# A row of maxima in another PSUM ring and one step earlier, the first weight loads three steps later, and a split of weights without its shift

## The chip, the cores and the metric

The kernel runs on one core of one Trainium2 chip. The time is device microseconds (us) of one launch. A profiled execution gives the trace, in which PE is TensorE's matmuls, PEld its weight loads, DVE is VectorE, ACT is ScalarE, POOL is GpSimd and SP is the engine that issues the DMAs.

## The reference

Attention with rotary positions, then two feed-forward layers, on float32 data (the weights of the layers come as float64 and are read as pairs of 32-bit words):

```
B, H, S, D = 4, 8, 576, 64                      # 32 heads
q, k = rotate(q), rotate(k)
scores = q @ k.T / sqrt(D)
attn = exp(scores - max(scores)) / (sum + 1e-9)
x = attn @ v                                    # to 2304 tokens x 512
x = (sigmoid(x @ w_gate) * (x @ w_val)) @ w_out      # 512 -> 1536 -> 512
x = elu(x @ w_in) @ w_out2                           # 512 -> 2048 -> 512
```

## The kernel before, in words

Products that need more than the fast matmul's precision are made of three: high by high, high by low part, low by high. So each operand is split into a high part (a cast on ACT) and a low part (a difference on DVE or POOL).

**Attention.** The order of the work is written out by hand as an agenda. A slot is one head (32 of them), and a slot has ten steps. In each step PE makes one tile of scores for head i (`scores`, L448: two matmuls into one bank of the ring `ps_qk`, of three banks), one tile of raw scores for head i+2 whose row maxima DVE takes (`maxima`, L400, ring `ps_mt` of two banks), and one step of the product with v for the scores of five steps ago (`values`, L475). ACT turns each tile of scores into its exponential (L468), which frees the bank. In steps 4 and 9 the tile is a tail of 64 rows; ACT writes its exponential twice (L465 and, in place, L468) and DVE takes a difference (`low_part`, L471, a step and a half later), which frees that bank. `at(slot, step, f)` puts f behind the work of a step; a step of ".5" puts it ahead of the next step's scores. What is put at one step goes out in the order in which the `at` calls stand.

**The maxima's row.** `join` (L416, at step 0 of the slot before) brings the maxima of a head together in MJ, `max_row` (L428) turns them into a row by a matmul with the identity (L434), DVE casts the row to SBUF (L436), and SP sends it by DMA into the operand W that the scores of the next head read (L441, or L443 and L444). For heads from 4 on this stands at step 2.5. Its bank is the one bank of `ps_t`, which for pairs of heads from 4 on also takes the transposes of rotated q and k (`split`, L324; T, L337) at steps 4 and 9, whose casts are L344 (ACT) and L340 (DVE).

**Weights.** A generator (`split_all`, L148) loads the float64 weights by halves (L99, 512 KB each) and splits each word by DVE operations (L121 to L140), a cast on ACT and two operations on POOL. For the first chunk each `pull` issues one DVE operation: 14 pulls a half. The first pull issues two loads, and stands at step 0 of slot 5; two pulls a slot follow, at steps 2 and 5 of slots 6 to 29, and the rest one a step from slot 30 on. Later chunks are split during the feed-forward layers, by 8 pulls a half.

**Feed-forward layers.** PE works through tokens in blocks of 512, with two rings of four banks; DVE adds each product to an accumulator (y L728, z L762), which frees the bank.

Of the kernel before, what the change touches and what calls it, by code (L numbers as in the profile page):

```python
# [9 lines left out]
F32 = mybir.dt.float32  # L10
F32R = mybir.dt.float32r
AF = mybir.ActivationFunctionType
ALU = mybir.AluOpType
AX = mybir.AxisListType
I32 = mybir.dt.int32
I64 = mybir.dt.int64


@with_exitstack
def attention_moe_moe_kernel(  # L20
# [15 lines left out]
    nc = tc.nc  # L36
    B, H, S, D = q.shape
    P = 128
# [55 lines left out]
    def load_w(c, n, half):  # L94
        w, view, parts = chunks[c][n]
        n2 = parts // 2
        place = sum(len(halves(j)) for j in range(1, c)) + 2 * n + half
        t = pools["raw", c > 0 and place % 4 > 1].tile([P, n2, DM if view is by_f else FC], I64, tag="raw", name=f"raw{c}_{n}{half}")
        nc.sync.dma_start(out=t, in_=view(w, c if c < NC1 else c - NC1)[:, half * n2 : (half + 1) * n2])  # L99
        raw_w[c, n, half] = t  # L100

    def split_w(c, n, half):

        t = raw_w.pop((c, n, half))
        shape = [P, 2 * t.shape[1], t.shape[2]]
        if half == 0:
            hi = pools["w", c % 2].tile(shape, F32R, tag="wh", name=f"wh{c}_{n}")
            lo = pools["w", c % 2].tile(shape, F32R, tag="wl", name=f"wl{c}_{n}")
            weights.setdefault(c, []).append((hi, lo))
        flat = lambda a: a.rearrange("p k f -> p (k f)")  # L110
        words = flat(t).bitcast(I32).rearrange("p (f two) -> p f two", two=2)
        size = NK * FC // 2
        for j in range(0, size, WP):
            low, high = words[:, j : j + WP, 0], words[:, j : j + WP, 1]
            h, l = (flat(x)[:, half * size + j : half * size + j + WP] for x in weights[c][n])
            e = pools["cv"].tile([P, WP], I32, tag="e", name=f"ce{c}_{n}{half}_{j}")
            m = pools["cv"].tile([P, WP], I32, tag="m", name=f"cm{c}_{n}{half}_{j}")
            a = pools["cv"].tile([P, WP], F32, tag="a", name=f"ca{c}_{n}{half}_{j}")
            mf = m.bitcast(F32)

            nc.vector.tensor_scalar(e, high, 20, 0x7FF, op0=ALU.logical_shift_right, op1=ALU.bitwise_and)  # L121
            if c == 0:
                yield
            nc.vector.tensor_scalar(m, high, 0x07FFFFFF, 3, op0=ALU.bitwise_and, op1=ALU.logical_shift_left)
            yield
            nc.vector.scalar_tensor_tensor(
                m, in0=high, scalar=-0x40000000, in1=m, op0=ALU.bitwise_and, op1=ALU.bitwise_or
            )
            if c == 0:
                yield  # L130
            nc.vector.scalar_tensor_tensor(a, in0=e, scalar=896.5, in1=mf, op0=ALU.is_gt, op1=ALU.mult)  # L131
            yield

            nc.vector.tensor_single_scalar(e, low, 8, op=ALU.logical_shift_right)
            if c == 0:
                yield
            nc.vector.tensor_single_scalar(m, a.bitcast(I32), -0x00800000, op=ALU.bitwise_and)  # L137
            nc.scalar.copy(h, a)  # L138
            yield
            nc.vector.scalar_tensor_tensor(mf, in0=e, scalar=2.0**-44, in1=mf, op0=ALU.mult, op1=ALU.mult)  # L140
            nc.gpsimd.tensor_tensor(out=a, in0=a, in1=h.bitcast(F32), op=ALU.subtract)  # L141
            yield
            nc.gpsimd.tensor_tensor(out=l, in0=a, in1=mf, op=ALU.add)  # L143

    def halves(c):
        return [(c, n, half) for n in range(len(chunks[c])) for half in range(2)] if c < NCH else []

    def split_all(which, ring):  # L148

        for one in which[:ring]:  # L150
            load_w(*one)
        yield
        for n, one in enumerate(which):
            yield from split_w(*one)
            if n + ring < len(which):
                load_w(*which[n + ring])
        yield
# [28 lines left out]
    with ExitStack() as att:  # L186
# [11 lines left out]
        ps_qk = banks.enter_context(tc.tile_pool(name="ps_qk", bufs=3, space=bass.MemoryType.PSUM))  # L198
        ps_t = banks.enter_context(tc.tile_pool(name="ps_t", bufs=1, space=bass.MemoryType.PSUM))
# [88 lines left out]
        def at(slot, step, fn, *args):  # L288
            agenda.setdefault(slot * NSTEP + step, []).append((fn, args))
# [3 lines left out]
        def rope_ops(pr, which, eng):  # L293


            if which == "t":
                x = raw(pr, "kq")
                r = rope_p.tile([P, 2, D], F32, tag="rt", name=f"rt{pr}")
                s = rope_p.tile([P, 2, D], F32, tag="st", name=f"st{pr}")
                rv, sv = r, s  # L300
                cos, sin = (tabt[:, j].unsqueeze(1).to_broadcast([P, 2, D]) for j in range(2))
            else:
                x = raw(pr, which)
                r = rope_p.tile([P, ST, 2, D], F32, tag="r" + which, name=f"r{which}{pr}", bufs=2)
                s = rope_p.tile([P, ST, 2, D], F32, tag="s", name=f"s{which}{pr}")
                rv, sv = (y.rearrange("p t h d -> p h t d") for y in (r, s))
                cos, sin = (tab[:, c].unsqueeze(1).to_broadcast([P, 2, ST, D]) for c in range(2))
            rot[pr, which] = r
            tt = eng.tensor_tensor

            axes = "p n" if which == "t" else "p h t"
            two = lambda y: y.rearrange(f"{axes} (two d) -> {axes} two d", two=2)
            tt(out=two(sv), in0=two(x)[..., ::-1, :], in1=two(sin), op=ALU.mult)
            yield
            tt(out=rv, in0=x, in1=cos, op=ALU.mult)
            yield
            tt(out=r, in0=r, in1=s, op=ALU.add)
            yield
# [97 lines left out]
        def join(i):  # L416
            pr, ab = divmod(i, 2)
            c = slice(ST + 1, 2 * ST + 1) if ab else slice(0, ST + 1)
            nc.vector.tensor_reduce(
                out=MJ[pr % 2][:, c], in_=MX[pr % 2][:, :, c].rearrange("p a t -> p t a"), axis=AX.X, op=ALU.min  # L420
            )
# [6 lines left out]
        def max_row(i):  # L428
            pr, ab = divmod(i, 2)
            mj = MJ[pr % 2]  # L430
            if i == 0:
                join(i)
            m = ps_t.tile([P, 512], F32, tag="t", name=f"mr{i}")[:, 0:P]
            nc.tensor.matmul(m, lhsT=mj[:, ST * ab : ST * ab + P], rhs=ident_r, start=True, stop=True)  # L434
            row = s_p.tile([ST + 1, P], F32R, tag="row", name=f"row{i}")
            nc.vector.tensor_copy(row, m[0 : ST + 1])  # L436
            z = D * (1 - ab)
            w, src = W[pr % NPAR][ab][z : z + 1, 3 * S :].bitcast(F32), row.bitcast(F32)
            by_p = lambda x: x.rearrange("o (t p) -> o t p", p=P)
            if ab == 0:  # L440
                nc.sync.dma_start(out=by_p(w), in_=src)  # L441
            else:
                nc.sync.dma_start(out=by_p(w[:, 0:SM]), in_=src[1 : ST + 1])  # L443
                nc.sync.dma_start(out=w[:, SM:S], in_=src[0:1, TL:P])  # L444
# [103 lines left out]
        for i in range(1, NHEAD):  # L548
            at(i - 1, 0, join, i)
        for i in range(NHEAD):  # L550
            at(*((i - 2, 9) if i == 0 else (i - 1, 1.5 if i < 4 else 2.5)), max_row, i)

        for qt in QT + MJ:
            at(-6, 0, nc.vector.memset, qt.bitcast(F32), 0.0)
# [4 lines left out]
        for pr, which, eng in ((0, "k", nc.vector), (0, "t", nc.gpsimd), (0, "q", nc.vector), (1, "k", nc.gpsimd), (1, "t", nc.gpsimd), (1, "q", nc.gpsimd)):  # L559
            gen = rope_ops(pr, which, eng)  # L560
# [18 lines left out]
        for pr in range(NPAIR):  # L579
            s0 = 2 * pr  # L580
            if pr > 1:
                for j, (which, slot, steps) in enumerate(
# [6 lines left out]
                    gen = rope_ops(pr, which, nc.gpsimd)  # L589
# [33 lines left out]
            at(NHEAD - 2, 1 + 2 * kk, lambda: pull(split_x[0]))  # L623

        gen = split_all(halves(0), 2)
        at(5, 0, pull, gen)
        pulls = 14 * len(halves(0)) + 1
        early = [(slot, step) for slot in range(6, NHEAD - 2) for step in (2, 5)]
        for slot, step in early:
            at(slot, step, pull, gen)  # L630
# [4 lines left out]
        for n in range(-6 * NSTEP, NHEAD * NSTEP + half_slot):  # L635
            i, h = divmod(n, NSTEP)
# [132 lines left out]
    for c in range(NCH):  # L769

        hooks = (4 + 4) * NB if c < NC1 else 2 * NB + NT // P
        pulls = 8 * len(halves(c + 1)) + 1
# [65 lines left out]
```

## Time and profile before

| | |
|---|---|
| median of 3 runs | 1174.69 us (1174.68 to 1175.4) |
| profiled execution, own time | 1177.32 us |
| its span, first to last instruction | 1175.5 us |
| busy: PE, DVE, ACT, POOL | 1141.1, 933.1, 448.9, 605.3 us |
| granted TensorE clock, mean | 0.999 of full speed (2.4 GHz) |

The attention takes the first 328 us or so, the two layers the rest. Busy time of PE is near the whole span; what counts is where PE waits and for whom.

### The profile page before, as it was taken

The page shows a single profiled execution, that of the slowest core. Times are in us where ns is not written, and L with a number is a line of the kernel's source. Part 1 is how long each engine was busy: PE and PEld are TensorE (multiplying, and loading weights), DVE is VectorE, ACT ScalarE, POOL GpSimd, SP SyncE. Part 2 cuts the span into 40 slices and gives each one's busy share as a digit, 9 for nine tenths or more (in the row PEclk, how much of TensorE's full clock was granted, in tenths as well). Part 3 has the DMA queues.
Part 4 walks back from the last instruction along what each step waited for, and adds up shares of the span by engine and source line. Part 5 has one row for each costly group of instructions (what it writes and reads, how often), then busy time and mean ns, then how long its engine had stood idle before and what let it go on. Part 6 is the DMA issues. An engine that isn't in the chain of part 4 may idle for free.

```text
span 1175.5 us, 16864 instructions
## 1 busy us (share of the span) xinstructions
PE 1141.1 (97%) x5728; PEld 962.9 (82%) x5728; DVE 933.1 (79%) x1994; ACT 448.9 (38%) x1037; POOL 605.3 (51%) x695
## 2 busy tenths in 40 slices
PE   5999999999999999999999999999999999999998
PEld 4887887788888888888888888888888888888887
DVE  6768778878776897767777677688999999999844
ACT  4666666666754332212222122344322222222221
POOL 8665758564243554434444445675545544544521
PEclk9999999999999999999999999999999999999999
DMA  6567676765312111111111111011111101110004
GB/s 168 145 157 179 151 181 140 186 153 133 80 48 94 54 54 55 37 54 37 54 37 47 44 37 36 18 37 54 38 52 37 54 36 55 36 47 9 1 36 126
DMA packets 58758, 88.03 MB, mean 75 GB/s; under 512 B 18176, under 2 KB 30736, under 8 KB 58672
## 3 DMA queue, kind: packets, MB, share of 16 engines
q1 hardware_dynamic: 58672, 86.96, 27.5%
q8 instruction: 45, 0.74, 0.3%
q14 instruction: 41, 0.34, 0.1%
HBM read 55.45 MB, written 4.87 MB: 51 GB/s over the span
## 4 chain that ended last, share of the span: by engine, by line
PE 76%; DVE 17%; ACT 3%; POOL 2%; issue 1%; DMA 1%; SPq 1%; POOLq 0%; ACTq 0%
PE h L680 12%; PE h L679 12%; PE h L681 12%; PE o L679 8%; PE o L680 8%; PE o L681 8%; PE pv L491 6%; PE s L461 5%; DVE z L762 3%; DVE MX L414 2%; PE mt L412 2%; DVE g L705 1%; DVE g L704 1%; DVE ca L131 1%; DVE hl L340 1%
## 5 line engine op out<-in xcount | busy, mean ns | idle before, releaser
L711 POOL TENSOR_TENSOR gl<-g,gh 128x512 fp32r<-128x512 f32 (+1 forms) x140 | 168.6, 1204 | 330.1 <-ACT gh L710 263.8
L710 ACT CAST gh<-g 128x512 fp32r<-128x512 f32 (+1 forms) x140 | 81.0, 579 | 307.6 <-DVE g L705 171.0
L461 PE MATMUL s<-W 128*128 128x288 f32 (+1 forms) x640 | 186.5, 371 | 3.0 <-DMA W<-row 1.7
L680 PE MATMUL h<-xl,wh 128*128 128x512 f32 (+1 forms) x480 | 176.6, 368 | 0.0
L679 PE MATMUL h<-xh,wh 128*128 128x512 f32 (+1 forms) x480 | 176.6, 368 | 0.0
L681 PE MATMUL h<-xh,wl 128*128 128x512 f32 (+1 forms) x480 | 176.5, 368 | 0.0
L414 DVE TENSOR_REDUCE MX<-mt 128x1 f32<-128x288 f32 x288 | 127.0, 449 | 50.5 <-PE mt L412 49.3
L491 PE MATMUL pv<-e,VF 128*128 128x288 f32 x512 | 166.5, 408 | 0.0
L141 POOL TENSOR_TENSOR ca<-ca,wh 128x256 f32<-128x256 f32 x136 | 111.3, 818 | 98.1 <-DVE cm L137 75.6
L461 PEld LDWEIGHTS s<-W 128*128 128x128 f32 (+1 forms) x640 | 109.9, 183 | 28.8 <-ACT e L468 2.6
L138 ACT CAST wh<-ca 128x256 fp32r<-128x256 f32 x136 | 55.1, 405 | 194.9 <-DVE ca L131 194.9
L468 ACT ACTIVATE e<-s 128x288 f32<-128x288 f32 x256 | 104.5, 412 | 43.3 <-PE s L461 40.4
L143 POOL TENSOR_TENSOR wl<-ca,cm 128x256 fp32r<-128x256 f32 x136 | 110.9, 815 | 18.8 <-DVE cm L140 13.0
L680 PE MATMUL h<-yl,wh 128*128 128x512 f32 (+1 forms) x320 | 117.7, 368 | 0.0
L681 PE MATMUL h<-yh,wl 128*128 128x512 f32 (+1 forms) x320 | 117.7, 368 | 0.0
L679 PE MATMUL h<-yh,wh 128*128 128x512 f32 (+1 forms) x320 | 117.7, 368 | 0.0
L679 PE MATMUL o<-wh,gh 128*128 128x512 f32 x288 | 112.7, 391 | 1.4 <-DVE z L762 1.1
L700 DVE TENSOR_TENSOR g<-h,g 128x512 f32<-128x512 f32 (+1 forms) x60 | 38.2, 636 | 94.9 <-PE h L681 92.1
L680 PE MATMUL o<-wl,gh 128*128 128x512 f32 x288 | 112.2, 390 | 0.0
L681 PE MATMUL o<-wh,gl 128*128 128x512 f32 x288 | 112.1, 389 | 0.0
L680 PEld LDWEIGHTS h<-xl,wh 128*128 128x128 f32 x480 | 90.5, 189 | 15.0
L681 PEld LDWEIGHTS h<-xh,wl 128*128 128x128 f32 x480 | 90.5, 189 | 15.0
(110 smaller groups left out, 2521.9 us busy)
## 6 DMA issues: line engine op xcount, KB each, us to landing
W<-hl SPq DMA_DIRECT2D x90, 288.0 KB
raw<-in_moe_w_out_dram SPq DMA_DIRECT2D x28, 512.0 KB
raw<-in_moe_w_in_dram SPq DMA_DIRECT2D x16, 512.0 KB
raw<-in_moe_w_gate_dram SPq DMA_DIRECT2D x12, 512.0 KB
raw<-in_moe_w_val_dram SPq DMA_DIRECT2D x12, 512.0 KB
rb<-d SPq DMA_DIRECT2D x32, 144.0 KB
k<-in_k_dram SPq DMA_DIRECT2D x16, 256.0 KB
q<-in_q_dram SPq DMA_DIRECT2D x16, 256.0 KB
```

Of the source, the lines that this page charges most:

```text
L138: nc.scalar.copy(h, a)
L141: nc.gpsimd.tensor_tensor(out=a, in0=a, in1=h.bitcast(F32), op=ALU.subtract)
L143: nc.gpsimd.tensor_tensor(out=l, in0=a, in1=mf, op=ALU.add)
L414: nc.vector.tensor_reduce(out=MX[pr % 2][:, a, c : c + 1], in_=m, axis=AX.X, op=ALU.max, negate=True)
L461: nc.tensor.matmul(s, lhsT=operand(i, st, t * P, n), rhs=operand(i, mv, a * HS, HS), start=st == "K1", stop=st == "K2")
L468: nc.scalar.activation(e, s, AF.Exp, scale=SCALE)
L491: nc.tensor.matmul(out_ps, lhsT=VF[par][:, ab, t], rhs=e, start=t == 0, stop=False)
L679: nc.tensor.matmul(ps, lhsT=ah, rhs=bh, start=j == 0, stop=False)
L680: nc.tensor.matmul(ps, lhsT=ah, rhs=bl, start=False, stop=False)
L681: nc.tensor.matmul(ps, lhsT=al, rhs=bh, start=False, stop=j == n - 1)
L710: nc.scalar.copy(hi, g)
L711: nc.gpsimd.tensor_tensor(out=lo, in0=g, in1=hi.bitcast(F32), op=ALU.subtract)
```

## The change

Four edits. The row's matmul takes a bank of the scores' ring `ps_qk` in place of `ps_t`. For all heads from 1 on it stands at step 1.5 (it was 2.5 for heads from 4 on). The shift of the low word (L134) goes: the operation behind it reads the low word in place, as an unsigned number, with the scale 2^-52 in place of 2^-44 (the eight low bits were cut off before, and are now kept). So a half takes 12 pulls, and the generator's first pull moves from step 0 to step 3 of slot 5; the later loads of the first chunk then come in slots 12, 18, 24 and 30 (they came in slots 13, 20, 27 and 30).

```
-            nc.vector.tensor_single_scalar(e, low, 8, op=ALU.logical_shift_right)
-            if c == 0:
-                yield
             nc.vector.tensor_single_scalar(m, a.bitcast(I32), -0x00800000, op=ALU.bitwise_and)
             nc.scalar.copy(h, a)
             yield
-            nc.vector.scalar_tensor_tensor(mf, in0=e, scalar=2.0**-44, in1=mf, op0=ALU.mult, op1=ALU.mult)
+            nc.vector.scalar_tensor_tensor(
+                mf, in0=low.bitcast(U32), scalar=2.0**-52, in1=mf, op0=ALU.mult, op1=ALU.mult
+            )
...
-            m = ps_t.tile([P, 512], F32, tag="t", name=f"mr{i}")[:, 0:P]
+            m = ps_qk.tile([P, 512], F32, tag="qk", name=f"mr{i}")[:, 0:P]
...
-            at(*((i - 2, 9) if i == 0 else (i - 1, 1.5 if i < 4 else 2.5)), max_row, i)
+            at(*((i - 2, 9) if i == 0 else (i - 1, 1.5)), max_row, i)
...
-        at(5, 0, pull, gen)
-        pulls = 14 * len(halves(0)) + 1
+        at(5, 3, pull, gen)
+        pulls = 12 * len(halves(0)) + 1
```

PE's order in slot 17 before, from the scores of step 2 to the transpose of step 4 (s_2 is the tile of scores of step 2, mr the row's matmul, Tk the transpose; a name in brackets is whose semaphore the row waits for):

```order
L461 MATMUL s_2_2826<-W_163 128x288 [waits Activation_49]
L461 MATMUL s_2_2826<-W_163 128x288
L412 MATMUL mt_2_2830<-W_165 128x288 [waits DVE_49]
L491 MATMUL pv_1_2800<-e_7_2749,VF_166 128x288
L434 MATMUL mr_2837<-identr,MJ_173 128x128 [waits DVE_49,PE_49]
L461 MATMUL s_3_2843<-W_163 128x288 [waits Activation_49]
L461 MATMUL s_3_2843<-W_163 128x288
L412 MATMUL mt_3_2847<-W_165 128x288 [waits DVE_49]
L491 MATMUL pv_1_2800<-e_8_2761,VF_166 128x288
L337 MATMUL Tk_0_2853<-ident,rk_2664 128x128 [waits DVE_49,Pool_49]
```

The same place in the changed kernel:

```order
L434 MATMUL mr_2825<-identr,MJ_173 128x128 [waits DVE_49,Activation_49]
L461 MATMUL s_2_2831<-W_163 128x288 [waits Activation_49]
L461 MATMUL s_2_2831<-W_163 128x288
L412 MATMUL mt_2_2835<-W_165 128x288
L491 MATMUL pv_1_2800<-e_7_2749,VF_166 128x288
L461 MATMUL s_3_2844<-W_163 128x288 [waits DVE_49]
L461 MATMUL s_3_2844<-W_163 128x288
L412 MATMUL mt_3_2848<-W_165 128x288 [waits DVE_49]
L491 MATMUL pv_1_2800<-e_8_2761,VF_166 128x288
L337 MATMUL Tk_0_2854<-ident,rk_2669 128x128 [waits PE_49,Pool_49]
```

The row's matmul stands ahead of the scores of step 2, and waits for ACT too, since its bank was one of scores; the transpose no longer waits for DVE. In the ring of three banks, one is held by the tail of the step before until DVE's difference, and the row now takes one: by the values that the semaphores wait for, s_2 takes the bank of s_1, and waits for the exponential of step 1 (it waited for that of step 0). In the slots 3, 6, 8, 12, 16, 20, 24 and 28 to 30 it takes the tail's bank, and waits for DVE's difference. From s_3 on the banks are two or more tiles old again, as before.

SP's order in slot 5, before (rk, hl and row are sources in SBUF, raw the weights as they come):

```order
L99 DMA raw_00_1082<-in_moe_w_gate_dram 128x2x256
L99 DMA raw_01_1084<-in_moe_w_gate_dram 128x2x256
L521 DMA r_1032<-d_1_1031 128x9
L441 DMA W_164<-row_1114 1x5x128
L524 DMA d_1_1031<-r_1032 128x9
```

And changed:

```order
L441 DMA W_164<-row_1100 1x5x128
L521 DMA r_1032<-d_1_1031 128x9
L100 DMA raw_00_1123<-in_moe_w_gate_dram 128x2x256
L100 DMA raw_01_1125<-in_moe_w_gate_dram 128x2x256
L524 DMA d_1_1031<-r_1032 128x9
```

The row of head 6 and the sums r go out ahead of the two loads of weights; the reciprocals (d from r) stay behind them.

## Rows read from the trace of the kernel before

**Rows 1.** By stage: length, busy us (x instructions) of PE, PEld, DVE, ACT, POOL, clock, DMA.

```profile
28.00:328.00 300.00, 285.46 (x1685) 244.61 (x1685) 233.23 (x594) 196.52 (x525) 179.51 (x237) 1.00 0.62 149
328.00:850.00 522.00, 522.00 (x2520) 441.38 (x2519) 402.88 (x808) 156.39 (x316) 255.17 (x269) 1.00 0.15 46
850.00:1075.00 225.00, 223.61 (x1038) 186.17 (x1038) 212.98 (x434) 60.50 (x128) 113.56 (x121) 1.00 0.13 43
```

**Rows 2.** Waits, 28 to 330 us: us in total, times, longest.

```profile
PE Tk L337 <- DVE row L436: 5.4, 10, 1.3
PE Tq L337 <- DVE row L436: 4.4, 7, 1.1
...
DVE r L523 <- DMA r<-d: 4.0, 3, 3.5
...
PE s L461 <- DMA W<-row: 1.7, 2, 1.5
...
PE Tq L337 <- POOL st L313: 1.1, 2, 0.7
```

**Rows 3.** Timeline of slot 17: start, duration, engine, line, operation.

```profile
192.71 0.64 PE L461 MATMUL s<-W 128*128 128x288 f32 x2
192.78 0.15 DVE L419 TENSOR_REDUCE MJ<-MX 128x5 fp32r<-128x10 f32 x1
192.81 0.41 ACT L468 ACTIVATE e<-s 128x288 f32<-128x288 f32 x1
...
193.59 0.44 PE L434 MATMUL mr<-identr,MJ 128*128 128x128 f32 x1
...
193.86 0.47 PE L461 MATMUL s<-W 128*128 128x288 f32 x2
...
194.84 0.27 DVE L436 CAST row<-mr 5x128 fp32r<-5x128 f32 x1
...
195.25 0.30 PE L337 MATMUL Tk<-ident,rk 128*128 128x128 f32 x1 [0.30 <-DVE row L436]
...
196.43 0.30 PE L412 MATMUL mt<-W 128*128 128x288 f32 x1
```

**Rows 4.** The same view, slot 22.

```profile
241.97 0.65 PE L461 MATMUL s<-W 128*128 128x288 f32 x2
...
242.29 0.83 ACT L468 ACTIVATE e<-s 128x288 f32<-128x288 f32 x2
```

**Rows 5.** The same view, slot 8.

```profile
104.42 0.45 DVE L471 TENSOR_TENSOR p<-s,p 64x288 fp32r<-64x288 f32 x1
...
104.80 0.65 PE L461 MATMUL s<-W 128*128 128x288 f32 x2
...
107.89 0.43 DVE L414 TENSOR_REDUCE MX<-mt 128x1 f32<-128x288 f32 x1
...
108.11 0.30 PE L337 MATMUL Tq<-ident,rq 128*128 128x128 f32 x1 [1.06 <-DVE row L436]
```

**Rows 6.** The same view, slots 5 and 6.

```profile
76.82 1.37 SPq L99 DMA_DIRECT2D raw<-in_moe_w_gate_dram  x1
...
80.44 0.82 SPq L441 DMA_DIRECT2D W<-row  x1
...
84.45 0.19 PEld L461 LDWEIGHTS s<-W 128*128 128x128 f32 x1 [1.69 <-DMA W<-row]
```

**Rows 7.** One line's instructions (L134, L140, L126): duration ns min/median/max, first and last start.

```profile
L134 DVE TENSOR_SCALAR ce<-raw x136: 275/284/1358, 106.7 to 1104.6; 128x256 int32<-128x256 int32 x136
...
L140 DVE SCALAR_TENSOR_TENSOR cm<-ce,cm x136: 407/426/1543, 116.8 to 1105.6; 128x256 f32<-128x256 int32 x136
...
L126 DVE SCALAR_TENSOR_TENSOR cm<-raw,cm x136: 406/426/1539, 97.2 to 1102.1; 128x256 int32<-128x256 int32 x136
```

**Rows 8.** Waits, 850 to 1160 us.

```profile
PE o L679 <- DVE z L762: 1.1, 2, 0.9
...
PE o L679 <- ACT g L703: 0.3, 1, 0.3
```

More of the change, by code (lines that the diff above doesn't have):

```diff
@@ L16 @@
 I64 = mybir.dt.int64
+U32 = mybir.dt.uint32
 @with_exitstack
```

## The prediction, made before the changed kernel was run

> **What bounds the kernel now.** I read the busy time by stage first. PE is busy without a gap from 328 to 850 us, and waits 1.4 us in all between 850 and 1075; in the attention it waits 14.5 of 300 us, and DVE there is 78% busy [rows 1]. So PE sets the end everywhere, and an edit is worth what it takes from PE's waits or adds to them. The waits by name come next: of the 14.5 us, 9.8 us in 17 waits are transposes T that wait for DVE's cast of the maxima's row, and two more waits of 1.1 us are put down to POOL, but sit at the same instruction; 1.7 us are scores that wait for the DMA of such a row [rows 2]. Last I read the timeline of three slots, to see what stands around that row. In slot 17 the row's matmul starts at 193.59, but DVE casts it at 194.84 only, behind the maxima of step 2 and an operation on weights; the cast ends at 195.11, and T, which needs the same bank, starts at 195.25 [rows 3]. From the end of an operation on another engine to PE's start it is thus 0.14 us; I use that below.
>
> **The change part by part.** The sum is made against the profiled execution (1177.32 us, its span 1175.5 and 1.8 around it). The runs' median, 1174.69, is 2.6 us below; I take the difference over to it.
>
> *The row leaves T's bank.* T then finds its bank free since the last transpose, five steps back. What goes: 5.4 + 4.4 + 1.1 = 10.9 us, 19 waits [rows 2]. What is late next there? T also needs POOL's rotated operand, issued ahead of it by several steps; and PE's next need of DVE is the maximum of step 3, whose bank the raw scores of step 5 take. In slot 8, the longest but one of these waits, T started at 108.11, and that maximum ran from 107.89 to 108.32 [rows 5]; with 0.14 it lets PE go on at 108.46. The raw scores of step 5 come 1.18 us behind T (195.25 to 196.43 [rows 3]), so T may come as early as 107.28 before DVE holds PE there instead. That caps the gain of one slot at 0.83 us. Only two slots reach it: this one (1.06) and the longest (1.3, less the new wait below). Cost of the cap: 0.2 + 0.1 = 0.3 us.
>
> *The row enters the scores' ring, a step earlier.* Now the scores of step 2 follow the row's matmul and take the bank of the scores of step 1, so they wait for ACT's exponential of step 1. In slot 17: they started at 192.71; the row's matmul ahead of them costs 0.27 (193.59 to 193.86), which it cost behind them before, so they want to start at 192.98. The exponential runs from 192.81 to 193.22, and lets them go at 193.36: a wait of 0.38 us [rows 3]. The row's own wait ends up at the same moment: MJ is ready at 192.93, the matmul could go at 193.07 and the scores at 193.34. In slot 22 the first of the two exponentials ends at 242.29 + 0.83/2 = 242.70; they want to go at 242.24 and may at 242.84: 0.60 us [rows 4]. I went through all slots in that way. Twelve odd slots (5, 7, 9 and so on to 27) are like slot 17, 0.33 to 0.39 each; six even ones (4, 10, 14, 18, 22, 26) are like slot 22, 0.57 in the mean; ACT is later there because its cast of the transposed k is larger. In the other slots the bank is that of the tail, and DVE's difference is in time: in slot 8 it ends at 104.87, which gives 105.01, and the scores want 104.80 + 0.27 = 105.07 [rows 5]. So the new wait is 12 x 0.38 + 6 x 0.57 = 8.0 us. Nothing hides it, since all of PE's later work stands behind the scores. No such wait is in the trace. From below it is bounded by nothing, as in the slots of slot 8's kind; from above by two whole exponentials more in each of the 18 slots, 18 x 2 x 0.41 = 14.8, so 22.8 us. I take 8.0, since up to the scores of step 1 both kernels issue the same work, and the exponential's end is read, not guessed. The cast of the row moves ahead of one maximum and the operation on weights on DVE; nothing else there changes place.
>
> *The first loads.* In slot 5 the two loads (1 MB) were issued from 76.82 on, the row of head 6 behind them at 80.44, and the scores that read it were held until 84.45, PE for 1.5 us [rows 6]. Now the row, cast about 76.5, and the sums r go first. That wait goes, and with it DVE's 3.5 us for r [rows 2], during which PE went on. The other 0.2 us of the 1.7 came behind a later load, which now comes after the row too. So 1.7 us go. What is queued behind the loads now: the reciprocals' store and the moves of pair 4, which PE first reads a full slot later, some 9 us, against the 3.6 us that the row took behind the same loads, measured from its issue (80.44 to 84.0). The loads of slots 12, 18 and 24 stand behind that slot's row and ahead of the broadcast of reciprocals, on which POOL alone waits. I cost this at nothing; were the broadcast late, POOL's rotations would be, which are about a slot ahead of T.
>
> *No shift.* 136 operations of DVE go; the middle one takes 284 ns, so at least 38.6 us of DVE. The operation that now reads the low word with a step of two words had a contiguous source; another of its kind that already reads with that step takes the same 426 ns [rows 7]. The unsigned reading is not in the trace: at best it costs nothing, at worst as much as the shift gave, 38.6 us of DVE. I take nothing. On the path that sets the end this counts only where PE waits for DVE in the layers: 1.1 + 0.3 us [rows 8], where DVE is 95% busy [rows 1]; the shifts are spread from 106.7 to 1104.6 us [rows 7], so that far more of their 38.6 us falls into that stage than PE waits there. So 1.4 us go at most, and I take them; otherwise the relief is hidden beside PE. In the attention the number of DVE operations a slot stays at two.
>
> The sum: -10.9 + 0.3 + 8.0 - 1.7 - 1.4 = -5.7 us, so 1171.6 for a profiled execution, and **1169.0 us** beside the median.
>
> The Trainium skill (Perfetto Trace Analysis, Optimization Strategy) says that a gap which repeats on the engine that should be saturated can mean that there are too few buffers for the next tile. It speaks against putting one more tile into a ring of three, and for the second rival below; the trace of before bears it out for a ring of one, by the 17 waits of T.
>
> **The rivals.**
>
> *The new wait doesn't bind.* If the exponential of step 1 is done in time, the 8.0 us stay away: -13.7, 1161.0 us. For it: in slots without a transpose's cast on ACT it is nearly so. Against it: the rows of slots 17 and 22, in which ACT is busy from the tail on.
>
> *The ring of three becomes a ring of one.* With a tail's bank and the row's bank both held, the scores of steps 1 and 2 share one bank, and if those of step 3 also come late (they take the tail's bank, behind DVE's difference and the maxima ahead of it) ACT and PE take turns instead of overlapping. That is an exponential more, 0.41 us, at step 3 and another at step 4 in the 18 slots: the wait becomes 22.8, the sum +9.1, and the time 1183.8 us. The change is a loss from a new wait of 13.7 us on, 0.76 us a slot. Against it: DVE's difference ended 0.06 us before it was wanted in slot 8 even at step 2, and at step 3 there are 0.9 us more.
>
> *DVE is the bound, and the wait only moves.* The cast was late because DVE was; if the maxima of steps 3 and 4 are as late, half of T's 10.9 us come back at the raw scores: -0.3, 1174.4 us. For it: DVE 78% busy, with operations on weights that stretch to 1.4 us. Against it: the 1.18 us of slack worked out above.
>
> **How the numbers follow.** The forecast 0.58; the new wait that doesn't bind 0.14; the ring of one 0.13; DVE 0.15. What a measurement of this kernel can tell from no change is about 0.2%, 2.3 us, so faster means below 1172.3 and slower above 1177.0; and a milder form of the ring's case lies between. Of the forecast 0.05 lie within the bound, of the ring's case 0.02, of DVE's case 0.11, with 0.02 to either side. Faster: 0.53 + 0.14 + 0.02 = 0.69; slower 0.11 + 0.02 = 0.13; same 0.18. The forecast's own range, with its wait between 5 and 11 us, is 1166 to 1172; the range that holds 8 of 10 reaches into the first rival and to the edge of the slower one: 1161.5 to 1175.5.
>
> **What would show it.** Right: the waits of T for the row are gone; PE's scores wait for ACT's exponential in some 18 slots, 0.3 to 0.6 us each, at step 2; no scores wait for a row's DMA; the layers' waits of PE for z are gone; slots 8, 12, 16, 20 and 24 shorten by nearly all of their old wait, slots like 11 and 22 hardly or not. Wrong: the raw scores wait for maxima instead (DVE), the scores wait at steps 3 and 4 too (the ring), or the attention ends more than 10 us earlier (the wait doesn't bind).

## The result and the profile after

The changed kernel takes **1164.97 us** (median of 4 runs, 1163.47 to 1165.68) against 1174.68 us of the kernel before in the same comparison: ratio 0.9919, 95% interval 0.9902 to 0.9936, or 9.7 us less. The forecast was 1169.0 us. The sign came out as predicted, and the time lies in the range given for 8 of 10 (1161.5 to 1175.5), 1 us below the narrower one that the forecast had for itself (1166 to 1172). Most of the places were right; two sizes were off, and a cost in slots 30 and 31 was missed.

The first view is again the busy time by stage (columns as in [rows 1]), of the kernel after:

```profile
28.00:328.00 300.00, 294.42 (x1728) 253.06 (x1727) 240.36 (x610) 203.99 (x538) 185.79 (x240) 1.00 0.63 150
328.00:850.00 522.00, 522.00 (x2518) 441.36 (x2518) 381.81 (x719) 153.33 (x308) 255.53 (x269) 1.00 0.15 47
850.00:1075.00 225.00, 225.00 (x1050) 188.71 (x1049) 206.80 (x403) 64.41 (x131) 116.13 (x122) 1.00 0.13 40
```

PE's idle time from 28 to 328 us falls from 14.5 to 5.6 us (the stretch now takes in some 10 us of the layers), and between 850 and 1075 us it is gone. DVE has 21 us less to do between 328 and 850, where PE was busy throughout before and after; that part of the relief is worth nothing, as forecast. The waits of PE from 28 to 330 us, which answer to [rows 2]:

```profile
PE s L461 <- ACT e L468: 2.8, 8, 0.8
PE s L461 <- DVE p L471: 1.4, 1, 1.4
PE mt L412 <- DVE MX L414: 1.0, 3, 0.4
PE Tq L337 <- DVE MX L414: 0.2, 1, 0.2
```

T no longer waits for the row, and no scores wait for a row's DMA. From 850 us on the view holds no wait of PE (before: [rows 8]). But by this view the scores' wait for the exponential has 2.8 us in 8 places, two of them in slot 30, not 8.0 in 18. The timeline of slot 17 shows why that is too little. Of the kernel before, three rows that were not shown yet:

```profile
190.89 0.29 PE L488 MATMUL pv<-p,VT 128*64 128x288 f32 x1
...
194.30 0.65 PE L491 MATMUL pv<-e,VF 128*128 128x288 f32 x2
...
195.90 0.30 PE L488 MATMUL pv<-p,VT 128*64 128x288 f32 x1
```

and the same slot of the kernel after (it answers to [rows 3]):

```profile
182.65 0.30 PE L488 MATMUL pv<-p,VT 128*64 128x288 f32 x1
...
184.19 0.65 PE L491 MATMUL pv<-e,VF 128*128 128x288 f32 x2
184.54 0.15 DVE L419 TENSOR_REDUCE MJ<-MX 128x5 fp32r<-128x10 f32 x1
184.56 0.41 ACT L468 ACTIVATE e<-s 128x288 f32<-128x288 f32 x1
...
184.84 0.30 PE L434 MATMUL mr<-identr,MJ 128*128 128x128 f32 x1
185.03 0.54 PE L461 MATMUL s<-W 128*128 128x288 f32 x2
...
186.41 0.65 PE L491 MATMUL pv<-e,VF 128*128 128x288 f32 x2
186.89 0.27 PE L337 MATMUL Tk<-ident,rk 128*128 128x128 f32 x1
187.51 0.29 PE L488 MATMUL pv<-p,VT 128*64 128x288 f32 x1
```

Without a wait T starts 0.48 us after the product with v (pv) begins (186.41 to 186.89), though that product's record is 0.65 long: its modelled end lies 0.17 us behind the moment at which PE could go on. Before, the distance was 0.95 (194.30 to 195.25), so T's wait had cost 0.47 us, and the idle column of [rows 3] showed 0.30. The same holds for the row after: it starts 0.65 us behind pv, just where pv's record ends, so that the view shows no idle time, and yet it is late.

So I measured by distances from start to start. The product with a tail (L488) stands twice in each slot; from one to the next is half a slot. The first half holds the row and the transposes of step 4; in slot 17 it took 195.90 - 190.89 = 5.01 us before and 187.51 - 182.65 = 4.86 after. Added up over the profiled executions (us; "rest" runs from the last of them but one to the end of the span):

| | before | after | ring alone | step alone | shift alone | loads alone |
|---|---|---|---|---|---|---|
| start to the first tail | 36.47 | 35.12 | 35.42 | 33.62 | 36.09 | 33.51 |
| slots 1 to 3 | 27.86 | 27.37 | 27.38 | 27.88 | 27.86 | 27.86 |
| slots 4 to 29, first halves | 136.49 | 124.66 | 126.88 | 130.22 | 134.70 | 132.82 |
| slots 4 to 29, second halves | 112.33 | 114.03 | 113.04 | 112.68 | 113.76 | 112.88 |
| slots 30 and 31 | 15.45 | 17.83 | 15.46 | 15.46 | 17.80 | 15.47 |
| rest | 846.90 | 844.19 | 846.92 | 846.94 | 844.19 | 846.86 |

The gain is in the first halves (-11.8) and in the rest (-2.7); 1.7 us come back in the second halves, and 2.4 in slots 30 and 31, which nothing in the prediction has. The first line differs between runs of kernels that do the same up to there (33.5 to 36.5), so it is no part of the change.

The new wait, by distances: after the change the first halves come in three sizes. Twelve odd slots take 4.86 us (4.64 in slot 27), six even ones (4, 10, 14, 18, 22, 26) take 5.08, and slots 6, 8, 12, 16, 20 and 24 take 4.58, the classes that the prediction named. Only in the even six does idle time show; slot 22, which answers to [rows 4]:

```profile
231.47 0.65 PE L491 MATMUL pv<-e,VF 128*128 128x288 f32 x2
...
231.74 0.44 PE L434 MATMUL mr<-identr,MJ 128*128 128x128 f32 x1
...
232.00 0.41 ACT L468 ACTIVATE e<-s 128x288 f32<-128x288 f32 x1
...
232.47 0.53 PE L461 MATMUL s<-W 128*128 128x288 f32 x2 [0.29 <-ACT e L468]
```

The scores start 0.06 us behind the end of ACT's exponential (232.00 + 0.41 = 232.41), as they do in all 18 slots (0.05 to 0.06). The prediction had reckoned with 0.14, read from a cast of DVE.

In slots 5 and 6 SP now issues the row (75.44) ahead of the loads, and the scores no longer wait for it (against [rows 6]):

```profile
75.44 1.18 SPq L441 DMA_DIRECT2D W<-row  x1
76.71 1.34 SPq L521 DMA_DIRECT2D r<-d  x1
78.11 1.76 SPq L100 DMA_DIRECT2D raw<-in_moe_w_gate_dram  x2
```

And the operation that reads the low word as an unsigned number with a step of two takes 426 ns, what it took before with a contiguous source [rows 7]:

```profile
L138 DVE SCALAR_TENSOR_TENSOR cm<-raw,cm x136: 407/426/1572, 104.8 to 1089.0; 128x256 f32<-128x256 uint32 x136
```

The new loss stands in slots 30 and 31, where, before and after, one pull of the weights' split is issued in each step, beside the split of the first tokens (xh on ACT, xl on DVE). Rows of ACT, PE and DVE of the kernel after:

```profile
306.91 0.41 ACT L136 CAST wh<-ca 128x256 fp32r<-128x256 f32 x1 [0.94 <-DVE ca L132]
...
307.68 0.53 PE L461 MATMUL s<-W 128*128 128x288 f32 x2 [0.76 <-ACT e L468]
...
308.17 0.69 DVE L172 TENSOR_TENSOR xl<-x,xh 128x512 fp32r<-128x512 f32 x1 [0.96 <-ACT xh L171]
...
313.53 0.40 ACT L136 CAST wh<-ca 128x256 fp32r<-128x256 f32 x1 [2.03 <-DVE ca L132]
...
314.36 0.40 PE L461 MATMUL s<-W 128*128 128x288 f32 x1 [1.35 <-DVE p L471]
```

ACT's cast (L136) stands one pull behind the DVE operation that makes its source; the shift between them is gone. ACT waits for that source, the exponentials and the token cast stand behind it in ACT's queue, and DVE then waits for ACT.

### The profile page after: what moved, and what is told of

The parts are those of the page before. It is cut to its first block, busy times and chain, and to the rows that moved or that the text cites. A ratio compares the mean times of both kernels' runs of the same rounds, so it can differ in the third digit from the quotient of the medians.

```text
span 1163.2 us, 16704 instructions
## 1 busy us (share of the span) xinstructions
PE 1139.7 (98%) x5728; PEld 964.0 (83%) x5728; DVE 898.0 (77%) x1858; ACT 452.9 (39%) x1037; POOL 606.7 (52%) x695
## 4 chain that ended last, share of the span: by engine, by line
PE 94%; DVE 2%; ACT 2%; issue 0%; SPq 0%; POOL 0%; DMA 0%; POOLq 0%
PE h L680 14%; PE h L679 14%; PE h L681 14%; PE o L680 10%; PE o L679 10%; PE o L681 10%; PE pv L491 9%; PE s L461 7%; PE mt L412 3%; DVE MX L414 1%; PE Tk L337 1%; PE pv L488 1%; PE pv L489 1%; PE Tq L337 1%; ACT e L468 1%; ACT hl L344 0%
## 5 line engine op out<-in xcount | busy, mean ns | idle before, releaser
L136 ACT CAST wh<-ca 128x256 fp32r<-128x256 f32 x136 | 55.1, 405 | 188.4 <-DVE ca L132 188.3
L143 POOL TENSOR_TENSOR wl<-ca,cm 128x256 fp32r<-128x256 f32 x136 | 111.2, 818 | 19.1 <-DVE cm L138 13.7
L679 PEld LDWEIGHTS h<-xh,wh 128*128 128x128 f32 x480 | 90.5, 189 | 15.1
```

Of the source, the lines that this page charges most:

```text
L679: nc.tensor.matmul(ps, lhsT=ah, rhs=bh, start=j == 0, stop=False)
```

## The experiments

Theory A, formed from the table above: the row's move out of T's bank is worth half as much again as the idle column said, the new wait about what was predicted, and removing the shift gives 2.7 us in the layers and takes 2.4 away in slots 30 and 31. The rivals: the prediction's own terms hold, or another of the edits makes the gain. Each kernel was timed beside the kernel before, whose median was 1174.39 us for the first four, then 1175.15 (four), 1175.47 (three) and 1174.97 (the last). Differences in us are differences of medians; the ratios, with their 95% intervals, need not be the quotient of the two medians.

### Each part of the change by itself

The row's ring and step alone (the shift, 14 pulls and the loads as before):

```
-            m = ps_t.tile([P, 512], F32, tag="t", name=f"mr{i}")[:, 0:P]
+            m = ps_qk.tile([P, 512], F32, tag="qk", name=f"mr{i}")[:, 0:P]
-            at(*((i - 2, 9) if i == 0 else (i - 1, 1.5 if i < 4 else 2.5)), max_row, i)
+            at(*((i - 2, 9) if i == 0 else (i - 1, 1.5)), max_row, i)
```

> Only the row's matmul goes into the scores' ring, with its step (1.5 for every head); the shift and the place of the first loads stay as before. Theory A (the two ring terms were both mis-sized, since a wait right behind a value matmul lies partly under that matmul's modelled end): by step intervals of the two traces T loses 16.4 us of waits in slots 4 to 28 and 2.0 in slots 0 and 1, the new wait gives back 6.2 and DVE's maxima 1.7, so -10.5 us: about 1164 us, nearly the whole gain. Theory B (the prediction's terms hold): -10.9 + 0.3 + 8.0 = -2.6 us, 1172 us, and the rest of the measured gain comes from the other parts.

Measured: 1167.36 us, ratio 0.9943 (0.9931 to 0.9955), so -7.0 us. The prediction's -2.6 is excluded; theory A's -10.5 is too much. Its table column shows -9.6 in the first halves. But that is against one profile of the kernel before: the two kernels that leave the row as it was have first halves shorter by 1.8 (shift alone) and, less the 1.76 of slot 6, by 1.9 us (loads alone). That profile had about 2 us more of T's waits than those two, and -9.6 + 0.7 - 0.5 + 1.9 = -7.5 agrees with the time.

The step alone (the second line of that diff, the row still in T's bank):

> Only the step of the row's matmul changes (1.5 instead of 2.5 for heads 4 to 31); the row stays in T's bank. Theory A (the ring is what pays, since T still has to wait for a cast that DVE reaches late): T's waits shrink by part of a step only, -3 us or less, 1172 us or more. Rival (the earlier step alone pays): the cast comes up to 0.88 us earlier, the 19 waits of T have a mean of 0.57, so most of them go, and no wait for an exponential is added: -9 us or more, 1166 us or less, and the ring is not needed.

Measured: 1169.12 us, 0.9963 (0.9950 to 0.9975), -5.3 us by the medians and -4.3 by the ratio: between the two. The earlier row ends T's waits here as well, but now the row itself waits in T's bank, for DVE's difference of the last transpose:

```profile
PE mr L434 <- DVE hl L340: 5.1, 12, 0.4
PE s L461 <- DMA W<-row: 1.3, 1, 1.3
```

Its even first halves take 5.24 us, against 4.58 where nothing waits. So the step alone gives most of what ring and step give together: 5.3 of 7.0 us by the medians, 4.3 of 6.7 by the ratios.

The shift alone (`L134` removed, the low word read as `low.bitcast(U32)` with 2^-52, `12 * len(halves(0)) + 1` pulls):

> Only the shift is gone and the low words are read as unsigned numbers (12 pulls for each half matrix instead of 14). Theory A: the layers give 1.4 to 2.8 us, but at the attention's end ACT's cast of the weights now comes one pull behind its source instead of two, ACT waits for DVE there and the exponentials queue behind it, which costs up to 2.4 us in slots 30 and 31: net -0.4 us, 1174.3, no difference that can be told. Theory B (the prediction): -1.4 us, 1173.3. Rival (DVE's relief also shortens T's waits in the attention): -4 us or more, 1170.7 or less.

Measured: 1174.52 us, 1.0001 (0.9992 to 1.0010): as theory A has it. The trace has both halves of it, +2.35 in slots 30 and 31 and -2.71 in the rest, and the same blocked queue:

```profile
318.13 0.40 ACT L136 CAST wh<-ca 128x256 fp32r<-128x256 f32 x1 [0.94 <-DVE ca L132]
...
325.57 0.53 PE L461 MATMUL s<-W 128*128 128x288 f32 x2 [1.36 <-DVE p L471]
```

The loads alone:

```
-        at(5, 0, pull, gen)
+        at(5, 3, pull, gen)
```

> Only the first loads of weights are issued three steps later. Theory A and the prediction alike: the wait of the scores for the row of head 6 goes, -1.7 us, 1173.0 us, and slot 6 loses its 2 us. Rival (the wait moves to another DMA behind the loads, the store of reciprocals or pair 4's moves): 0, 1174.7 us.

Measured: 1172.65 us, 0.9985 (0.9976 to 0.9993), -1.7 us, and the first half of slot 6 falls from 6.83 to 5.07. As forecast. The three parts add up to -7.0 + 0.1 - 1.7 = -8.6 us, against -9.7 for all together, within what the intervals allow.

### The new wait

The changed kernel with the row at step 2.5 again, still in the scores' ring:

```
-            at(*((i - 2, 9) if i == 0 else (i - 1, 1.5)), max_row, i)
+            at(*((i - 2, 9) if i == 0 else (i - 1, 1.5 if i < 4 else 2.5)), max_row, i)
```

> The changed kernel, with the row's matmul back at step 2.5 for heads 4 to 31 (still in the scores' ring). Theory A (the new wait belongs to the place of the row, not to the ring): behind the scores of step 2 the row finds MJ and the exponential of step 1 long done, so the 0.27 us of each odd slot and the 0.50 of six even ones go: -6.2 us against the changed kernel, about 1159 us; T does not wait again, since it no longer shares a bank with the row. Rival (with one tile more in a ring of three the wait only moves on, to the scores of step 3 behind DVE's difference or to step 4): 0, 1165 us, and the first halves of the slots keep their 4.86 and 5.08 us.

Measured: 1161.27 us, 0.9882 (0.9866 to 0.9897), 3.7 us below the changed kernel. The first halves of slots 4 to 26 fall to 4.51 us (odd) and 4.58 (even) in all but slot 8 (0.1 us more) and slots 12 and 20 (0.5 and 1.7 us more, where PE waits for DMAs); the row now starts 0.27 us behind pv:

```profile
184.75 0.65 PE L491 MATMUL pv<-e,VF 128*128 128x288 f32 x2
185.02 0.44 PE L434 MATMUL mr<-identr,MJ 128*128 128x128 f32 x1
185.29 0.47 PE L461 MATMUL s<-W 128*128 128x288 f32 x2
```

This gives the new wait its size: 4.86 - 4.51 = 0.35 in the odd slots, 5.08 - 4.58 = 0.50 in the even, 12 x 0.35 + 6 x 0.50 = 7.2 us. It was the place, as theory A had it; by the rival the first halves would have kept their sizes. But beside those two slots the second halves take 3.6 us back (117.58 against 114.03) in the profiled execution, which with 1163.94 us was the slowest of the four. The ring has a part in that, once: scores that wait for the row's cast, in slot 8. The larger part is raw scores that wait for maxima:

```profile
PE mt L412 <- DVE MX L414: 1.4, 4, 0.6
...
PE s L461 <- DVE row L436: 0.6, 1, 0.6
```

ACT's copy of the first half's sums two steps later, so that the exponential of step 1 starts earlier:

```
-            at(i + 1, 5 * a + 0.5, evacuate, *done, "s")
+            at(i + 1, 5 * a + 0.5 + 2 * (a == 0), evacuate, *done, "s")
```

> The changed kernel, with ACT's copy of the first half's sums two steps later (2.5 instead of 0.5), so that the exponential of step 1 ends up to 0.4 us earlier. Theory A (in the odd slots two waits end together, the row's for DVE's MJ and the scores' for the exponential): the odd slots keep 4.86 us, only the six even slots gain, -3.0 us at most, 1162 us. Rival (the prediction's term alone: the exponential of step 1 sets the wait everywhere): the wait goes in all 18 slots, -6.2 us, 1159 us.

Measured: 1162.00 us, 0.9889 (0.9873 to 0.9904); the interval touches that of the changed kernel, so the time alone tells little. The trace tells more, though its execution was the slowest of the four (1166.12 us): the six even slots fall from 5.08 to 4.62, the odd ones only from 4.86 to 4.76. In the even ones it is the exponential alone. In the odd ones two waits end nearly together, for the exponential and 0.1 us before it for MJ, as the prediction's own rows said [rows 3]; with the exponential out of the way the row still waits for MJ. Slot 17 of this kernel:

```profile
186.00 0.65 PE L491 MATMUL pv<-e,VF 128*128 128x288 f32 x2
...
186.35 0.15 DVE L419 TENSOR_REDUCE MJ<-MX 128x5 fp32r<-128x10 f32 x1
...
186.65 0.30 PE L434 MATMUL mr<-identr,MJ 128*128 128x128 f32 x1
```

The row starts 0.15 us behind the end of MJ (186.50), and 0.65 behind pv.

### Slots 30 and 31

ACT's cast of the first chunk one pull later:

```
-            nc.scalar.copy(h, a)
+            if c > 0:
+                nc.scalar.copy(h, a)
             yield
+            if c == 0:
+                nc.scalar.copy(h, a)
```

> The changed kernel, with ACT's cast of the weights' high part one pull later for the first part of the weights (beside the reading of the low words), so that it stands two pulls behind its source again, as it did before the shift was removed. Theory A (in slots 30 and 31 ACT waits for that source with the exponentials queued behind it): slots 30 and 31 lose the 2.35 us that they gained, -2.4 us, 1162.6 us. Rival (DVE is late there because of its own long operations, 0.96 and 0.70 us, not ACT's order): 0, 1165 us.

Measured: 1163.58 us, 0.9901 (0.9889 to 0.9914): not told from the changed kernel. Slots 30 and 31 lose 0.64 us, not 2.35. ACT still waits, since DVE itself is late, in an operation on two SBUF tiles that takes 1.13 us beside one of POOL (in this kernel lines behind the edit stand three further down, and L127 is L126 of the kernel before):

```profile
310.11 1.60 POOL L544 TENSOR_TENSOR x<-u,rb 128x320 f32<-128x320 f32 x2 [1.58 <-DMA rb<-d]
310.13 1.13 DVE L127 SCALAR_TENSOR_TENSOR cm<-raw,cm 128x256 int32<-128x256 int32 x1
...
311.30 0.70 DVE L132 SCALAR_TENSOR_TENSOR ca<-ce,cm 128x256 f32<-128x256 int32 x1
...
312.03 0.41 ACT L140 CAST wh<-ca 128x256 fp32r<-128x256 f32 x1 [1.35 <-DVE ca L132]
```

The Trainium skill (GPSIMD Engine Reference, Specifications) says that GpSimd shares its SBUF interfaces with VectorE and contends with VectorE's instructions that have two SBUF inputs; these rows agree, 1.13 and 0.70 us against the middle value of 0.43 [rows 7].

Row and cast together:

> The changed kernel with the row's matmul at step 2.5 and the cast one pull later, both. If both theories A hold and the two places are independent: -6.2 - 2.4 = -8.6 us against the changed kernel, 1156 us. If only the cast's holds: 1162.6; if neither: 1165.

Measured: 1159.44 us, 0.9876 (0.9858 to 0.9893): the row's gain, and 1.8 us more by the medians or 0.7 by the ratios, which the intervals don't tell from nothing. Slots 30 and 31 are 0.8 us shorter than with the row alone.

The row at step 2.5, and the last 25 pulls begun eight steps later, behind the token split:

```
-            at(NHEAD - 2, j, pull, gen)
+            at(NHEAD - 2, 8 + j, pull, gen)
```

> The row at step 2.5, and the 25 last pulls of the conversion begun eight steps later in slot 30, behind the split of the first tokens, which DVE and ACT have to do there too. Theory A (the 2.35 us lost in slots 30 and 31 come from ACT and DVE waiting for each other, where the split and the conversion run beside each other): slots 30 and 31 fall from 14.2 to about 11.9 us, 1159 us. Rival (the loss only moves behind slot 31, as the conversion ends later and the first layer's weights with it): 1161 us or more, with waits of PE for wh or wl at 320 us.

Measured: **1157.46 us**, 0.9848 (0.9831 to 0.9866), below both kernels. Slots 30 and 31 fall from 17.81 to 14.80, below the 15.45 of the kernel before, and the rest stays at 844.19: nothing moved behind. So the 2.4 us hang on the two splits running beside each other there, and the cast's distance is only a part of them. But the kernel before ran them beside each other too, with the shift, and took 15.45 us: what it is in the shorter chain that makes them cost so much more is not shown.

### What the late row gives back

Early pulls one in each even slot and three in each odd one, with the row at step 2.5:

```
-        early = [(slot, step) for slot in range(6, NHEAD - 2) for step in (2, 5)]
+        early = [(slot, step) for slot in range(6, NHEAD - 2) for step in ((2, 5, 8) if slot % 2 else (5,))]
```

> The row at step 2.5, and the early pulls of the weights' conversion dealt out as one in each even slot and three in each odd slot (before: two in each; 48 in all either way). With the row at step 2.5 the first halves of slots 4 to 29 lost 5.0 us against the changed kernel and the second halves gained 3.5, nearly all in even slots. Theory A (there the maxima wait for DVE, which runs out of time beside POOL's long operations, and a conversion's operation tips it): the second halves fall from 117.6 towards 112.4 us, 3 to 5 us less than the row alone: 1156 to 1158 us. Rival (DVE's work in the attention is the bound however it is dealt out): the waits turn up in the odd slots instead, 1161 us.

Measured: 1163.41 us, 0.9901 (0.9885 to 0.9917). Theory A falls: against the row alone the second halves get 3.8 us shorter, but the first halves 3.5 longer. The longest are those of even slots (8, 14 and 20), which the rival doesn't have either. With the late pulls added:

> The row at step 2.5, the early pulls one and three by turns, and the last pulls eight steps later. If both theories A hold: 1161.3 - 4 - 2.3 = 1155 us, some 10 us below the changed kernel. If one holds: 1157 to 1159. If neither: 1161.

Measured: 1160.95 us, 0.9871 (0.9850 to 0.9892), no better than the late pulls without it. Something else than the number of DVE operations holds some slots: in slot 20 scores wait 1.5 us for the row's DMA here, and 1.2 us without the late pulls. The waits of the kernel with the late row and pulls name two things:

```profile
PE s L461 <- DMA W<-row: 1.4, 2, 0.8
PE mt L412 <- DVE MX L414: 1.1, 5, 0.3
```

At step 2.5 the row's DMA is issued behind the gather of the sums (L521), which SP puts out at step 2, and lands too late for the next head's scores in slot 8:

```profile
94.55 0.77 SPq L521 DMA_DIRECT2D r<-d  x1
95.42 1.26 SPq L441 DMA_DIRECT2D W<-row  x1
...
98.87 0.40 PE L461 MATMUL s<-W 128*128 128x288 f32 x1 [0.84 <-DMA W<-row]
```

So the last kernel issues the row at the end of step 2, ahead of what else stands there; PE's order is the same:

```
-            at(*((i - 2, 9) if i == 0 else (i - 1, 1.5 if i < 4 else 2.5)), max_row, i)
+            at(*((i - 2, 9) if i == 0 else (i - 1, 1.5 if i < 4 else 2)), max_row, i)
```

> As the kernel with the late row and the late last pulls (1157.46 us), but the row's matmul is issued at the end of step 2 instead of just ahead of step 3: TensorE's order is the same, while DVE casts the row ahead of that step's operation on weights, and the row's DMA goes ahead of the loads and of the sums' moves that are issued there. Theory A (what the late row gave back in slots like 8, 14, 18 and 20 is partly the row's DMA behind 1 MB of loads or a late cast): the slots with 5.4 to 5.8 us fall to 4.58, the sum over both halves of slots 4 to 29 falls from 238.5 to about 236 us, and the time to 1155 us. Rival (DVE's maxima are the whole of it): 1157.5 us.

Measured: 1156.60 us, 0.9852 (0.9831 to 0.9874). Its waits from 28 to 330 us:

```profile
PE s L461 <- ACT e L468: 0.8, 2, 0.5
PE mt L412 <- DVE MX L414: 0.6, 2, 0.4
PE Tq L337 <- DVE MX L414: 0.2, 1, 0.2
```

The wait for the row's DMA is gone, and both halves of slots 4 to 29 take 231.5 us against 234.8; by the time alone it can't be told from the kernel of the late row and pulls, nor its rival excluded. Up to the first tail its profiled execution took 1.6 us more.

## Why the prediction was right, and where its sizes were off

- *The row leaves T's bank, -10.9 us: right in place and sign, mis-sized.* Against the 4.51 and 4.58 us of a first half in which nothing waits, the 26 first halves of the profile of before hold 19.1 us of waits; less 1.7 in slot 6 and 0.5 in slot 28 for rows' DMAs, some 16.8 are T's. The step that failed was to read the size of a wait from the idle column: 21 waits of T show 11.8 us there (the prediction counted 19 of them, 10.9; two put down to another operation of POOL were left out), and each hides at least the 0.17 us by which pv's record runs on, 3.6 in all. The other 1.4 us are waits too short to show. In the two other profiles with the row in its old place (shift alone, loads alone) it is about 2 us less.
- *The cap by DVE's maxima, +0.3: not told.* The second halves gave back 1.7 us between the two profiled executions, in slots 8, 12, 16 and 20 above all, and in 8, 12 and 20 the view shows raw scores that wait for a maximum. But in the table the three kernels that leave the row as it was have second halves of 112.33 to 113.76 us, and the three that move it 112.68 to 114.03: most of the 1.7 can be a difference between executions. The rival "DVE is the bound, and the wait only moves" thus has a tenth of T's 16.8 us for itself at most, not a half. The prediction's reading also missed a slot: a third wait, 0.91 us in slot 16, stood above the cap of 0.83.
- *The new wait, +8.0: right.* 7.2 us by distances, 0.35 in twelve odd slots and 0.50 in six even ones (0.38 and 0.57 were forecast), in the slots named; the scores start 0.06 us behind the exponential, not 0.14, which is about the difference. In the odd slots the exponential ends last by 0.1 us only, behind MJ. That PE's idle column would show it in some 18 slots was wrong: it shows the even six. The ring of three did not become a ring of one: the waits at steps 3 and 4 are not there.
- *The loads, -1.7: right.* -1.7 us by themselves.
- *No shift, -1.4: the net is near zero.* In the layers it gave 2.7 us, where the prediction had 1.4 us as the most, from the idle column; the starts of the layers' matmuls gain in three places (1.3, 0.6 and 0.9 us), where PE had shown waits of 0.93, 0.28 and 0.18 for z and g. In slots 30 and 31 it cost 2.4. The step that failed there is that the shift's removal was counted as relief alone, and its effect on the order between DVE and ACT was put at nothing, on the ground that the DVE operations a slot stay at two: that holds up to slot 29, and the two slots behind it, with a pull in every step, were not looked at. The unsigned reading cost nothing.

With these sizes the sum is -16.8 + 1.7 + 7.2 - 1.7 - 0.5 - 0.5 (slots 1 to 3) - 2.7 + 2.4 = -10.9 us against the profile of before, some 9 with those 2 us taken off, where 9.7 were measured. So the forecast's -5.7 came 4 us short because two errors of the same kind, both from the idle column, outweighed the costs it missed. That it came no less near is in part luck: the errors had opposite signs.

The Trainium skill (Perfetto Trace Analysis, Identifying the Most-Contended Engine) says that the matmuls' busy share is not a good measure of how close a kernel is to its roofline, and gives as the reason that pipelined instructions look smaller in the trace. The first bears on this error: PE showed 98% from 28 to 328 us after the change, and all but 1.7 of the new wait's 7.2 us lay within that. The second is the other way round in these rows, where a record lasts 0.65 us and PE can go on after 0.48.

## What to carry to other kernels

Size a wait by the distance between two starts, against the same piece of work where nothing waits; the idle column finds the wait, but it only begins where the record ahead of it ends. When an operation is taken out of a chain that runs across engines with queues in order, look at who now stands one step closer to its source, in each stage in which the chain is issued at another density. And move a tile within the order before moving it to another ring: the earlier step alone gave 5.3 of the 7.0 us (4.3 of 6.7 by the ratios), and the best kernel has the new ring and nearly the old place.

## What the hardware showed that was not expected

A fp32 matmul of 288 columns by two instructions has a record of 0.65 us, but the next instruction can start 0.48 us after it began. A DVE operation on two SBUF tiles took 1.13 us beside POOL's, against 0.43. That is no single case: in the changed kernel the 50 operations of L127 that run beside no operation of POOL take 0.40 to 0.43 us, and the 86 others up to 1.53. Operations with a single SBUF tile as source stretch too: those of L125 take 0.28 to 0.29 us without POOL, and up to 1.40 beside it. And the time up to the first tail differs by 3.0 us between executions that do the same there (33.5 to 36.5), more than several of the effects looked for, which is why the table keeps it apart.
